# First K and V on GpSimd's queue, ahead of the zero fills, and one late fill moved off SyncE's queue

## The chip, the cores and the metric

The kernel runs on one core of a Trainium2 chip. The metric is the device time of one execution in microseconds, the median of several. Executions of one kernel on one chip lie within about 0.4% of each other. All data movement of the core goes through 16 DMA engines. Three instruction streams start transfers on them: SyncE (queue q1 in the profile), GpSimd (q0, which the profile calls software_dynamic) and ScalarE (q10, little used here).

## The reference, cut

One decode step of a pre-norm transformer layer, forward and backward. Attention sees the last 4096 of 32768 cached positions, 8 K/V heads of 256:

```
k = k_cache[:, :, Sk - W:, :]; v = v_cache[:, :, Sk - W:, :]     # W = 4096, Sk = 32768
p = softmax(q @ k.T / 16);  h = x + (p @ v) @ wo
h2 = h + ((ln(h) @ w_gate) * (ln(h) @ w_up)) @ w_down
out = h2, and the gradients of x, k_cache, v_cache, wq, wo, w_gate, w_up, w_down
```

The gradients of the caches have the full shape (1, 8, 32768, 256) in bf16, and seven eighths of each are zeros. Writing 235 MB of zeros is most of this kernel's work.

## The kernel before

Zeros are written from one area of SBUF, `zeros` (128 x 8192 bf16, 16 KB a partition). Its second half is lent to a weight block for a while. The parts that matter, with cuts marked:

```python
    nc.vector.memset(ar(0, ZW // 2), 0.0)               # ZW = 8192; LD = nc.sync, ZQ = nc.gpsimd
    nc.gpsimd.memset(ar(ZW // 2, ZW // 2), 0.0)
    LD.dma_start(out=wqA, in_=wq_A)                     # query weights, 3.1 MB and 0.5 MB
    LD.dma_start(out=wqB, in_=wq_B)
    LD.dma_start(out=x_bf[:], in_=...)
    # ...
    late_jobs = [(out_2, G - 1, 5, 7, 2 * ZW), (out_3, G - 1, 0, 6, 2 * ZW), (out_3, G - 1, 6, 7, ZW)]
    # fills: 2 MB pieces, 7 to a (gradient, head); for head 7 only 5 pieces of out_2
    send_fills(0, HALF0)                 # 42 pieces in 6 DMAs of 14 MB, packets of 16 KB
    send_fills(HALF0, HALF1, True)       # 15 pieces from the first half of the source, packets of 8 KB
    # ...
    load_kv(K_off[0], A_k_cache, 0)      # on SyncE, 2.1 MB
    LD.dma_start(out=dh2_bc[:], in_=grad_out...)
    load_kv(V_off[0], A_v_cache, 0)
    # ... attention, then the gated block in three weight blocks:
    for n in range(len(BLOCKS)):
        # ... products of block n; block 1's gate and up weights lie in the second half of the zero source
        if n + 2 < len(BLOCKS):
            load_block(n + 2)
        if n == 1:
            nc.vector.memset(ar(ZW // 2, ZW // 2), 0.0)      # give the half back
            send_fills(HALF1, len(fills) - 1)                # the other 16 KB fills, on GpSimd
    # ... backward of attention; then the last fill in four odd DMAs, then on SyncE:
    for o, g, n0, n1, f in late_jobs:
        # ... zero fills behind the last outputs
```

Of the kernel before, what the change touches and what calls it, by code (L numbers as in the profile page):

```python
# [16 lines left out]
G = 8  # L17
Dh = 256
W = 4096
T = 32  # L20
# [3 lines left out]
Sk = 32768  # L24
EPS = 1e-5
SCALE = 1.0 / 16.0
ZW = 8192
HALF0, HALF1 = 42, 57
GROUP = 7
NZ = (Sk - W) * Dh // (128 * ZW)  # L30
KB = 512
# [3 lines left out]
def kernel(  # L35
        ctx, tc, A_x, A_k_cache, A_v_cache, A_wq, A_wo, B_x, B_w_gate, B_w_up, B_w_down, grad_out,
           out_0, out_1, out_2, out_3, out_4, out_5, out_6, out_7, out_8):
    nc = tc.nc
    LD = nc.sync
    ZQ = nc.gpsimd  # L40
# [10 lines left out]
    MB = UB + 48 * KB  # L51
# [3 lines left out]
    def ar(off, n):  # L55
        return arena[:, off:off + n]

    def kv_at(off):
        return ar(off, T * Dh).rearrange("p (t d) -> p t d", d=Dh)

    zeros = ar(0, ZW)
    A_off = [VB, VB + 32 * KB, UB + 32 * KB, UB, UB + 16 * KB, VB + 16 * KB]
    V_off = [A_off[i] for i in (0, 1, 2, 3, 4, 5, 0, 1)]
    K_off = [RB, RB + 32 * KB, MB + 16 * KB, RB, RB + 32 * KB, A_off[1], RB, RB + 32 * KB]
# [28 lines left out]
    dg_bc = ar(A_off[5], 2 * F).rearrange("p (i f) -> p i f", i=2)  # L93
    diag2 = ar(A_off[5] + 2 * F, F)

    nc.vector.memset(ar(0, ZW // 2), 0.0)
    nc.gpsimd.memset(ar(ZW // 2, ZW // 2), 0.0)
    x_bf = const.tile([1, D], bf16)
    dh2_bc = const.tile([128, D], bf16)
    wq_A = A_wq[0:384, :].rearrange("(c p) j -> p c j", c=3)  # L100
# [17 lines left out]
        reg = o[0, g, 0:Sk - W, :].rearrange("s d -> (s d)")[n0 * 128 * ZW:n1 * 128 * ZW]  # L118
        return reg.rearrange("(n p f) -> n p f", p=128, f=f)

    late_jobs = [(out_2, G - 1, 5, 7, 2 * ZW), (out_3, G - 1, 0, 6, 2 * ZW), (out_3, G - 1, 6, 7, ZW)]
    fills = []
    for g in range(G):
        for o in (out_2, out_3):
            if g == G - 1 and o is out_3:
                continue
            fills += [(o, g, i) for i in range(5 if g == G - 1 else NZ)]

    def send_fills(n0, n1, halves=False):
        while n0 < n1:  # L130
# [72 lines left out]
        nc.vector.scalar_tensor_tensor(out=r[:], in0=t[:], scalar=rstd, in1=plus, op0=ALU.mult, op1=ALU.add)  # L203
        return r

    def load_kv(off, cache, g):
        LD.dma_start(out=kv_at(off), in_=cache[0, g, Sk - W:, :].rearrange("(p t) d -> p t d", t=T))

    load_kv(K_off[0], A_k_cache, 0)
    LD.dma_start(out=dh2_bc[:], in_=grad_out.rearrange("a b d -> (a b) d").to_broadcast([128, D]))  # L210
    load_kv(V_off[0], A_v_cache, 0)
    load_kv(K_off[1], A_k_cache, 1)
    load_kv(V_off[1], A_v_cache, 1)

    dup = small.tile([1, 128], bf16, tag="dup", bufs=1)
    nc.vector.tensor_copy(out=dup[:].rearrange("o (m w) -> o m w", w=2), in_=x_bf[:, 384:D].unsqueeze(2).to_broadcast([1, 64, 2]))
# [18 lines left out]
                                 start=False, stop=(h == 1 and k == 2))  # L235
    qT_bf = const.tile([128, 32], bf16)
    nc.vector.tensor_copy(out=qT_bf[:], in_=qT_ps[:])
    load_kv(K_off[2], A_k_cache, 2)
    load_kv(V_off[2], A_v_cache, 2)

    pT_all = const.tile([128, G, T, 2], bf16)
    oT_f = const.tile([128, 2, H], f32)
# [30 lines left out]
    with tc.tile_pool(name="ps_m", bufs=1, space=bass.MemoryType.PSUM) as ps_m, \  # L273
# [43 lines left out]
        def moments(g, p_f):  # L317
            K_sb, V_sb = kv_at(K_off[g]), kv_at(V_off[g])
            M_ps = ps_m.tile([128, 2, 2 * Dh], f32, tag="M")
            for c in range(8):  # L320
                pK = pK_slot[c % 2]
                nc.vector.tensor_tensor(out=pK, in0=K_sb[:, 4 * c:4 * c + 4, :].unsqueeze(2).to_broadcast([128, 4, 2, Dh]),  # L322
                                        in1=p_f[:, c::8, :].unsqueeze(3).to_broadcast([128, 4, 2, Dh]), op=ALU.mult)
                for i in range(4):
                    t = 4 * c + i
                    for vh in range(2):
                        nc.tensor.matmul(M_ps[:, vh, :], lhsT=V_sb[:, t, vh * 128:(vh + 1) * 128], rhs=pK[:, i, :, :].rearrange("p h d -> p (h d)"),  # L327
                                         start=(t == 0), stop=(t == T - 1))
            for t in range(T):
                nc.tensor.matmul(ok_ps[:].rearrange("p k d -> p (k d)"), lhsT=ppad[g % 2][:, 8 * (t % 4) + t // 4, :], rhs=both(g, t),  # L330
                                 start=(g == 0 and t == 0), stop=(g == G - 1 and t == T - 1))
            for vh in range(2):
                nc.scalar.copy(out=M_sb[g][:, vh].rearrange("p h d -> p (h d)"), in_=M_ps[:, vh, :])  # L333

        def load_wo(n):
            LD.dma_start(out=wo_sb[:, 16 * n:16 * n + 16, :], in_=A_wo.rearrange("(p j) n -> p j n", j=32)[:, 16 * n:16 * n + 16, :])
# [4 lines left out]
        for g in range(G):  # L341
            p_f = p_next
            if g + 1 < G:
                p_next = scores(g + 1)
            moments(g, p_f)
            for kind, n in after.get(g, []):
                if kind == "K":
                    load_kv(K_off[n], A_k_cache, n)
                else:
                    load_kv(V_off[n], A_v_cache, n)  # L350
            if g == G - 2:
                load_wo(0)
        nc.vector.tensor_copy(out=ok_rows, in_=ok_ps[:])
# [151 lines left out]
    with tc.tile_pool(name="work2", bufs=2) as work2, tc.tile_pool(name="lnw", bufs=1) as lnw, \  # L505
# [10 lines left out]
                                     start=False, stop=(kh == 1))  # L516
            nc.scalar.activation(out=dq_bc[:, g * 512:(g + 1) * 512], in_=dqb_ps[:, 0, :], func=ACT.Copy, scale=SCALE)  # L517
        for g in range(2):
            load_kv(MB + 16 * KB * g, A_v_cache, g)

        HJ = H * Dh // 2
        dn1 = lnw.tile([128, 5], f32)
# [92 lines left out]
        for it, g in enumerate(order):  # L615
# [30 lines left out]
            for l in range(8):  # L646
                for qp in range(2):
# [5 lines left out]
                    t = 4 * l + 2 * qp  # L653
# [14 lines left out]
        o, g, i = fills[-1]  # L668
        flat = zero_rows(o, g, i, i + 1, ZW)[0].rearrange("p f -> (p f)")
        base = 0  # L670
        for p0, k, m, w in ((0, 5, 2, 288), (20, 3, 8, ZW), (64, 8, 9, ZW - 40), (0, 4, 8, ZW)):
            n = k * m * w
            ZQ.dma_start(out=flat[base:base + n].rearrange("(k m f) -> k m f", k=k, m=m),
                         in_=zeros[p0:p0 + 4 * k - 3:4, 0:w].unsqueeze(1).to_broadcast([k, m, w]))
# [35 lines left out]
```

## Time and profile before

| | kernel before |
|---|---|
| time, median | 793.49 us (793.19 to 794.0, 4 runs) |
| profiled execution | span 791.1 us |
| bytes moved | 334.75 MB: q0 216.01, q1 116.68 |
| rate in the long middle (60 to 300 us) | 430 GB/s |

The quantity used is **lost time**: a moment t, less the bytes moved until then divided by 430 GB/s. It is worked out from the packet records of the trace. A flat stretch of it is a stretch in which the DMA engines are full. As the rate hardly rises above 430 GB/s anywhere, a step is time that isn't made up later. The profile's lines are shown in the prediction below.

### The profile page before, as it was taken

To read this page: it belongs to the slowest core of one execution; us is meant where nothing else is said; L and a number is where in the kernel's file an instruction comes from. 1 tells how busy PE (TensorE), PEld (TensorE's weight loads), DVE (VectorE), ACT (ScalarE), POOL (GpSimd) and SP (SyncE) were. 2 spreads that over 40 slices of the span, in tenths; PEclk is the share of its full clock that TensorE was granted. 3 is DMA by queue.
4 is the path that set the end of the run, shared out by engine and by line. 5 is a ranking of instruction groups with operands and counts; after the bars stand their busy time and mean duration, and the time that the engine had idled before them with its cause. 6 is when DMAs were issued, how large, how long until landed. Compare 5 with 4: busy or idle time off the path is not lost.

```text
span 791.1 us, 7239 instructions
## 1 busy us (share of the span) xinstructions
PE 475.9 (60%) x2926; PEld 220.8 (28%) x2926; DVE 410.6 (52%) x621; ACT 196.1 (25%) x309; POOL 29.8 (4%) x41
## 2 busy tenths in 40 slices
PE   0359998999999999453226848583551535363100
PEld 0224333344343433142114714231210211131000
DVE  2105764847658476052884288486680583555300
ACT  0043123141241301000101207372331344134300
POOL 6000000000000000110300000000000000001000
PEclk9987999999999999655556959886556556556555
DMA  9999999999999999999999999999999999999998
GB/s 345 429 432 430 429 430 431 432 431 432 428 427 430 427 427 426 418 420 422 433 431 425 425 425 432 427 429 430 427 426 429 428 427 429 423 428 407 413 439 350
DMA packets 28759, 334.75 MB, mean 423 GB/s; under 512 B 1966, under 2 KB 5046, under 8 KB 6966
## 3 DMA queue, kind: packets, MB, share of 16 engines
q0 software_dynamic: 15904, 216.01, 64.2%
q1 hardware_dynamic: 11382, 116.68, 35.1%
q10 hardware_dynamic: 1440, 1.61, 0.6%
q8 instruction: 23, 0.38, 0.2%
q14 instruction: 10, 0.08, 0.0%
HBM read 53.69 MB, written 280.59 MB: 423 GB/s over the span
## 4 chain that ended last, share of the span: by engine, by line
another core or an unknown queue 40%; DMA 25%; DVE 14%; PE 10%; issue 2%; POOL 2%; ACT 1%; DVEq 0%; ACTq 0%; SPq 0%; POOLq 0%
DMA out_dram<-arena 25%; DVE arena L469 2%; PE rows_ps L266 2%; DVE arena L658 2%; DVE arena L554 2%; PE dqb_ps L512 2%; DVE arena L659 2%; PE d_ps L651 2%; PE tr_ps L263 1%; DVE arena L524 1%; DVE arena L438 1%; POOL out_dram L138 1%; PE dqb_ps L515 1%; DVE arena L623 1%
## 5 line engine op out<-in xcount | busy, mean ns | idle before, releaser
L322 DVE TENSOR_TENSOR arena<-arena,p_f 128x2048 bf16<-128x2048 bf16 x64 | 145.4, 2287 | 64.3 <-PE M_ps L327 64.2
L327 PE MATMUL M_ps<-arena 128*128 128x512 bf16 x512 | 129.3, 381 | 0.2 <-ACT arena L333 0.2
L651 PE MATMUL d_ps<-arena 32*128 32x512 bf16 x256 | 45.4, 521 | 100.6 <-DVE arena L659 85.7
L263 PE MATMUL tr_ps<-ident_bf,arena 128*128 128x128 bf16 x1024 | 92.2, 241 | 20.2 <-DMA arena<-in_A_k_cache_dram 12.7
L266 PE MATMUL rows_ps<-arena,vpad 128*16 128x512 bf16 x256 | 89.5, 445 | 21.4 <-DVE arena L623 15.9
L263 PEld LDWEIGHTS <-arena 128*128 128x128 bf16 x1024 | 68.3, 107 | 74.2 <-issue 60.3
L280 ACT COPY arena<-tr_ps 128x1024 bf16<-128x1024 bf16 x64 | 61.8, 1015 | 70.5 <-PE tr_ps L263 70.5
L330 PE MATMUL ok_ps<-arena 128*16 128x512 bf16 x256 | 64.0, 381 | 0.9 <-DVE arena L307 0.9
L655 ACT CAST arena<-d_ps 128x512 bf16<-128x512 f32 x64 | 37.7, 589 | 106.1 <-PE d_ps L651 106.1
L327 PEld LDWEIGHTS <-arena 128*128 128x128 bf16 x512 | 43.3, 99 | 59.2 <-issue 23.4
L621 ACT COPY arena<-tr_ps 128x1024 bf16<-128x1024 bf16 x32 | 32.5, 1016 | 109.9 <-PE tr_ps L263 35.8
L658 DVE CAST arena<-d_ps 128x512 bf16<-128x512 f32 x64 | 43.9, 686 | 18.2 <-PE d_ps L651 17.7
L659 DVE CAST arena<-d_ps 128x512 bf16<-128x512 f32 x64 | 43.6, 681 | 15.5 <-DMA out_dram<-arena 15.5
L651 PEld LDWEIGHTS <-arena 32*128 32x128 bf16 x256 | 10.7, 96 | 126.0 <-issue 81.9
L656 ACT CAST arena<-d_ps 128x512 bf16<-128x512 f32 x64 | 38.1, 595 | 16.8 <-DMA out_dram<-arena 16.8
L266 PEld LDWEIGHTS <-vpad 128*16 128x16 bf16 x256 | 18.7, 91 | 58.4 <-issue 50.6
L330 PEld LDWEIGHTS <-arena 128*16 128x16 bf16 x256 | 19.1, 89 | 41.6 <-issue 20.5
L549 DVE TENSOR_SCALAR arena<-arena,xT 128x1792 bf16<-128x1792 bf16 (+1 forms) x9 | 7.7, 881 | 37.1 <-DMA out_dram<-arena 37.1
L295 ACT ACTIVATE e_f<-cols_ps,nbias 128x32 f32<-128x32 f32 x16 | 4.5, 286 | 86.9 <-DVE nbias L291 86.9
L524 DVE CUSTOM_DVE_ANT_0 arena<-arena 128x4096 bf16<-128x4096 bf16 x3 | 13.1, 4421 | 23.7 <-ACT arena L517 23.7
L268 DVE COPY arena<-rows_ps 16x512 f32<-16x512 f32 x16 | 10.8, 676 | 27.7 <-PE rows_ps L266 27.7
L623 DVE COPY arena<-tr_ps 128x1024 bf16<-128x1024 bf16 x32 | 21.8, 683 | 3.0 <-PE tr_ps L263 2.5
(198 smaller groups left out, 382.2 us busy)
## 6 DMA issues: line engine op xcount, KB each, us to landing
out_dram<-arena POOLq DMA_DIRECT2D x11, 14336.0 KB, 196.1
out_dram<-arena SPq DMA_DIRECT2D x18, 2048.0 KB, 25.6
out_dram<-arena POOLq DMA_DIRECT2D x15, 2048.0 KB, 54.2
arena<-in_A_v_cache_dram SPq DMA_DIRECT2D x10, 2048.0 KB, 52.8
arena<-in_A_k_cache_dram SPq DMA_DIRECT2D x8, 2048.0 KB, 31.3
out_dram<-arena SPq DMA_DIRECT2D x4, 4096.0 KB, 26.1
out_dram<-arena POOLq DMA_DIRECT2D x1, 12288.0 KB, 43.0
out_dram<-arena POOLq DMA_DIRECT2D x1, 8192.0 KB, 337.3
```

Source lines behind the costliest of these rows:

```text
L263: nc.tensor.transpose(tr_ps[:, dh, i, :], X_sb[:, 4 * q + i, dh * 128:(dh + 1) * 128], ident_bf[:])
L266: nc.tensor.matmul(rows_ps[:], lhsT=pad[:, dh, 16 * q:16 * q + 16], rhs=XT[:, dh].rearrange("p t k -> p (t k)"), start=(q == 0 and dh == 0 ...
L280: sT_ps = dots(kv_at(K_off[g]), KT_slot, vpad[g % 2], rows1, ps_c, "cols", lambda q, XT, ps: nc.scalar.copy(out=XT, in_=ps))
L322: nc.vector.tensor_tensor(out=pK, in0=K_sb[:, 4 * c:4 * c + 4, :].unsqueeze(2).to_broadcast([128, 4, 2, Dh]), in1=p_f[:, c::8, :].unsqueez ...
L327: nc.tensor.matmul(M_ps[:, vh, :], lhsT=V_sb[:, t, vh * 128:(vh + 1) * 128], rhs=pK[:, i, :, :].rearrange("p h d -> p (h d)"), start=(t == ...
L330: nc.tensor.matmul(ok_ps[:].rearrange("p k d -> p (k d)"), lhsT=ppad[g % 2][:, 8 * (t % 4) + t // 4, :], rhs=both(g, t), start=(g == 0 and ...
L621: nc.scalar.copy(out=XT, in_=ps)
L651: nc.tensor.matmul(d_ps[:, qi].rearrange("p w d -> p (w d)"), lhsT=rTm[32 * q:32 * (q + 1), l, :], rhs=R_sb[32 * q:32 * (q + 1), :], start ...
L655: nc.scalar.copy(out=stV[:, t:t + 2, :], in_=d_ps[:, :, 0, :])
L656: nc.scalar.copy(out=stK[:, t:t + 2, :], in_=d_ps[:, :, 1, :])
L658: nc.vector.tensor_copy(out=stV[:, t:t + 2, :], in_=d_ps[:, :, 0, :])
L659: nc.vector.tensor_copy(out=stK[:, t:t + 2, :], in_=d_ps[:, :, 1, :])
```

## The change

The intent is to let K and V of head 0 arrive earlier by a queue that is otherwise waiting, and to keep GpSimd's queue running longer while the last outputs are computed. For that, one zero fill of 4 MB (pieces 5 and 6 of `out_2`, head 7; "the late fill" from here on) goes from SyncE's tail to GpSimd. The core of the diff (the other calls of `load_kv` only get the engine as an argument):

```diff
-    nc.vector.memset(ar(0, ZW // 2), 0.0)
-    nc.gpsimd.memset(ar(ZW // 2, ZW // 2), 0.0)
+    load_kv(ZQ, K_off[0], A_k_cache, 0)
+    load_kv(ZQ, V_off[0], A_v_cache, 0)
+    nc.vector.memset(zeros, 0.0)
...
-    late_jobs = [(out_2, G - 1, 5, 7, 2 * ZW), (out_3, G - 1, 0, 6, 2 * ZW), (out_3, G - 1, 6, 7, ZW)]
+    late_jobs = [(out_3, G - 1, 0, 6, 2 * ZW), (out_3, G - 1, 6, 7, ZW)]
...
-            fills += [(o, g, i) for i in range(5 if g == G - 1 else NZ)]
+            fills += [(o, g, i) for i in range(NZ)]
...
-    load_kv(K_off[0], A_k_cache, 0)
     LD.dma_start(out=dh2_bc[:], in_=grad_out...)
-    load_kv(V_off[0], A_v_cache, 0)
```

More of the change, by code (lines that the diff above doesn't have):

```diff
@@ L94, with load_kv @@
     diag2 = ar(A_off[5] + 2 * F, F)
-    nc.vector.memset(ar(0, ZW // 2), 0.0)
-    nc.gpsimd.memset(ar(ZW // 2, ZW // 2), 0.0)
+    def load_kv(eng, off, cache, g):
+        eng.dma_start(out=kv_at(off), in_=cache[0, g, Sk - W:, :].rearrange("(p t) d -> p t d", t=T))
+    load_kv(ZQ, K_off[0], A_k_cache, 0)
+    load_kv(ZQ, V_off[0], A_v_cache, 0)
+    nc.vector.memset(zeros, 0.0)
     x_bf = const.tile([1, D], bf16)
@@ L204, in layernorm_bwd @@
         return r
-    def load_kv(off, cache, g):
-        LD.dma_start(out=kv_at(off), in_=cache[0, g, Sk - W:, :].rearrange("(p t) d -> p t d", t=T))
-    load_kv(K_off[0], A_k_cache, 0)
     LD.dma_start(out=dh2_bc[:], in_=grad_out.rearrange("a b d -> (a b) d").to_broadcast([128, D]))
-    load_kv(V_off[0], A_v_cache, 0)
-    load_kv(K_off[1], A_k_cache, 1)
-    load_kv(V_off[1], A_v_cache, 1)
+    load_kv(LD, K_off[1], A_k_cache, 1)
+    load_kv(LD, V_off[1], A_v_cache, 1)
     dup = small.tile([1, 128], bf16, tag="dup", bufs=1)
@@ L237 @@
     nc.vector.tensor_copy(out=qT_bf[:], in_=qT_ps[:])
-    load_kv(K_off[2], A_k_cache, 2)
-    load_kv(V_off[2], A_v_cache, 2)
+    load_kv(LD, K_off[2], A_k_cache, 2)
+    load_kv(LD, V_off[2], A_v_cache, 2)
     pT_all = const.tile([128, G, T, 2], bf16)
@@ L347 @@
                 if kind == "K":
-                    load_kv(K_off[n], A_k_cache, n)
+                    load_kv(LD, K_off[n], A_k_cache, n)
                 else:
-                    load_kv(V_off[n], A_v_cache, n)
+                    load_kv(LD, V_off[n], A_v_cache, n)
             if g == G - 2:
@@ L518 @@
         for g in range(2):
-            load_kv(MB + 16 * KB * g, A_v_cache, g)
+            load_kv(LD, MB + 16 * KB * g, A_v_cache, g)
         HJ = H * Dh // 2
```

## The prediction

> **What bounds the kernel now.** I read the slices of the page first, then the queues, then the engines in stretches, and only then single instructions. The page says that the 16 DMA engines are busy in all 40 slices, and how many bytes they move:
>
> ```profile
> DMA  9999999999999999999999999999999999999998
> GB/s 345 429 432 430 429 430 431 432 431 432 428 427 430 427 427 426 418 420 422 433 431 425 425 425 432 427 429 430 427 426 429 428 427 429 423 428 407 413 439 350
> DMA packets 28759, 334.75 MB, mean 423 GB/s; under 512 B 1966, under 2 KB 5046, under 8 KB 6966
> ...
> q0 software_dynamic: 15904, 216.01, 64.2%
> q1 hardware_dynamic: 11382, 116.68, 35.1%
> ```
>
> The reader is to see 334.75 MB at about 430 GB/s, which is 778 us of pure moving, in a span of 791. So the kernel is bound by the sum of its bytes, and a change can only win or lose **time in which the DMA engines are not full**. Of the two queues, q0 is GpSimd's (zero fills, 216 MB) and q1 is SyncE's. The table by stretches says where the 12.6 us beyond 778 lie:
>
> ```profile
> 0.00:10.00 10.00, 0.37 (x1) 0.09 (x1) 4.55 (x18) 1.28 (x1) 9.41 (x14) 1.00 0.84 283
> 10.00:60.00 50.00, 18.72 (x224) 12.24 (x225) 4.60 (x21) 10.41 (x15) 2.64 (x4) 0.94 1.00 426
> 60.00:300.00 240.00, 235.00 (x1322) 95.64 (x1319) 153.16 (x139) 65.51 (x98) 3.41 (x5) 0.98 1.01 430
> 300.00:375.00 75.00, 41.33 (x248) 21.15 (x247) 26.68 (x60) 5.45 (x12) 5.46 (x8) 0.66 1.02 421
> ...
> 740.00:745.00 5.00, 0.76 (x8) 0.11 (x4) 2.58 (x4) 2.15 (x4) 0.00 (x0) 0.50 0.84 353
> 745.00:785.00 40.00, 0.00 (x0) 0.00 (x0) 0.00 (x0) 0.00 (x0) 0.00 (x0) 0.50 1.01 432
> 785.00:791.00 6.00, 0.00 (x0) 0.00 (x0) 0.00 (x0) 0.00 (x0) 0.00 (x0) 0.50 0.46 194
> ```
>
> The last two columns are DMA share and GB/s. At the start 283 against 430 for 10 us is 3.4 us lost; at 740 to 745, 0.9 us; at the end 3.3 us, the last transfers and their landing. TensorE is full from 60 to 300 (235 of 240 us), but no DMA waits for it there: zero fills take whatever rate the loads leave.
>
> One stage is fragile. The second half of the zero source is lent to a weight block, so GpSimd sends fills from the first half only (15 fills of 2 MB in 8 KB packets) until VectorE has zeroed the second half again. The timelines of TensorE, VectorE and GpSimd there:
>
> ```profile
> 372.34 0.74 PE L420 MATMUL gu_ps<-X_b,arena 64*128 64x1 bf16 x8 [1.67 <-DMA arena<-in_B_w_gate_dram]
> 381.23 1.76 DVE L443 MEMSET arena<- 128x2048 uint32 x1 [0.41 <-DVE hh_f L424]
> 383.29 5.71 POOL L142 DMA_DIRECT2D out_dram<-arena  x6 [30.72 <-DVE arena L443]
> ```
>
> Weights land at 372, the memset ends at 383.0, the next fills are issued at 383.3. The packet records show their first 16 KB packet at 389.7, while most engines finish their last 8 KB packet between 389.5 and 391.5. From 375 to 400 q1 carries nothing. So the new fills come with about one microsecond to spare: the same release some microseconds later leaves the DMA engines empty.
>
> **What the Trainium skill says.** "DMA: Bandwidth & Descriptors", section "Specifications", gives 435 GB/s as the ceiling of the fabric and about 358 GB/s as an HBM limit. The trace agrees with the first (430 held for hundreds of microseconds) and contradicts the second. The same page, "Issuing engines are not separate DMA queues": transfers started by scalar, sync or gpsimd run on the same 16 engines and interleave. The trace agrees (the shares of q0 and q1 add up to 99.3% of 16 engines), so moving a transfer to another queue buys no bandwidth. The same page, "Queues, rings and completion order": each engine takes turns between queues packet by packet. The trace agrees: between 16 and 20 us, q0 with 16 KB packets moves 328 GB/s beside q1 with mostly 4 KB packets at 108. Hence **small packets get a small share**. "Specifications" also gives about 1 us to the first byte of a GpSimd DMA; here it was 5.7 us (issued at 5.13, first q0 packet at 10.82), and 5.2 us at 715.
>
> **The change part by part.**
>
> (1) K and V of head 0 (2.1 MB each) leave q1 and go first into q0. They are issued at about 0.75 us, so with 5.5 us of latency they move from 6.3 us on. The bytes are the same. q1 alone already reached 430 GB/s from 4 to 7 us, so the only start time to be won is the dip from 7.5 to 12 us, where the rate fell to 246 to 311 GB/s: 0.6 MB, 1.4 us. If that dip comes from GpSimd's writing the fills' descriptors (5 to 12 us), it stays. I take **-0.7 us**.
>
> (2) The zero source is now cleared by VectorE alone: twice the 1.76 us memset, 3.5 us, ending near 4.8 instead of GpSimd's 4.25. Fills wait behind K and V anyway: 0.
>
> (3) The compute chain. Weights wq now share with 16 KB packets from 6.3 us, at one third of the rate (estimate 142 GB/s), so x and grad_out, queued behind them, come at about 25 (now 21) and 32 us (now 37.9, as K no longer stands ahead). In the built program TensorE now transposes K before this and waits for grad_out before the query product, so the first scores end near 47 (now 51). Then it gains more: now TensorE idles 5 us for the second K until 58.5, which will land near 42. The first weighted product of VectorE starts at 61.5 now, about 51 then: a **lead of 10 us**. By itself worth nothing, as the DMA is the bound.
>
> (4) The order of loads in the weight stage. The instruction order of the built program shows that the gate and up weights of block 1 (the ones in the borrowed half) now stand behind those of block 2 on SyncE's and ScalarE's queues. Block 2's wait for VectorE to be done with block 0 (issued at 355.4 now). So block 1's loads no longer run while block 0 is computed. With the lead of 10 us, shrunk to 8.5 by 16 KB fills that last until about 309, block 2's loads go out near 347, land after the 15 to 17 us they take now, near 364, and block 1's need another estimate of 11.6 us: 28 packets per engine in turn with an 8 KB fill packet, 0.415 us a turn. They land at 375. Then come the products of block 1 (2.7), broadcast and copies (5.2 in block 0 now), the four products of 1.23 (4.9) and the memset (1.8): **end at 389.5 instead of 383.0**.
>
> (5) What that costs. By bytes the 8 KB fills end at the same moment as now, 389.5 to 391.5, less the 0.7. New fills would flow from 389.5 + 5.5 = 395. The DMA engines stand idle for about **+5 us**, and nothing makes that up.
>
> (6) The late 4 MB fill leaves SyncE's tail (18.9 MB of q1 lie behind the last outputs, now from 743) and lengthens q0, which now ends at 730. That keeps DMA engines full while the last outputs are computed, so the dip at 740 to 745 should go: **-0.9 us**. The end itself stays.
>
> Sum: -0.7 + 5 - 0.9 = +3.4, so about 797.
>
> **The rivals.** *The intent works*: the weights land in time, there is no gap, and only -0.7 to -2.3 is left: 791 to 793. For it: the lead may be larger than 10 us, and 5 us more would close the gap; (4) is a sum of nine terms. Against it: the slack now is only about 1 us. *The gap is larger*: a lead of 5 us, or small packets that starve beside 16 KB fills, puts the memset at 395 and the gap at 10 us, 802; beyond 15 us would need the lead to vanish. *Compute becomes the bound at the end*: the chain leaves the weight stage some 6 us later than now, and q0 keeps half the rate until nearly 740, so the last outputs may come after q0 has run dry: +3 to +6 on top. Against: q0's extra 4.2 MB covers 10 us. *All hidden*: the start is shared differently and nothing else moves: 793.
>
> **Range and chances.** Everything here is a few microseconds out of 793; 2% is 15.9. The intent alone gives 791, the gap with a late tail about 803. I take 797 with 790 to 804. Faster by 2% needs 16 us of empty DMA time, and there are only 12.6 in all: 1%. Slower by 2% needs a gap of 17 us or more: 4%. Within 2%: 95%.
>
> **What would show it.** Right: the first q0 packets near 6 us, x later than 21 us, the first weighted product near 51, TensorE's waits for K shorter; in the weight stage a wait for the block 1 gate or up weights at about 375, the memset ending near 389, and a slice near 390 with a DMA share clearly under 9 and GB/s well under 420; no dip at 740. Wrong: the memset ending by 383 with full slices (the intent), or full slices near 390 and a hole near 740 (the tail). The prediction fails most likely at the lead of (3), or at how block 1's loads queue in (4).

## The result, and the profile after

The kernel after took **794.15 us** (median of 4, 793.5 to 794.7) against 793.49. The ratio is 1.0007 with a 95% interval of 0.999 to 1.0025. A ratio here is the mean time of one kernel's fast runs over that of the other's of the same rounds, so it is not quite the ratio of the medians. So the two kernels are the same within what can be measured. The page of the kernel after, its slices and its queues:

```profile
DMA  9999999999999999999999999999999999999997
GB/s 361 412 428 430 430 433 428 430 432 428 431 429 426 433 420 416 428 422 421 430 432 419 427 426 429 430 427 433 423 426 429 426 427 431 423 427 418 419 437 324
DMA packets 28871, 334.75 MB, mean 422 GB/s; under 512 B 1950, under 2 KB 5030, under 8 KB 6950
...
q0 software_dynamic: 16448, 224.40, 66.8%
q1 hardware_dynamic: 10950, 108.29, 32.4%
```

The same bytes, 8.4 MB of them on the other queue, and still full slices. The first slice is higher than before (361 against 345), the second lower (412 against 429): something was won and given back at once. The table by stretches:

```profile
0.00:10.00 10.00, 0.00 (x0) 0.00 (x0) 4.71 (x11) 1.28 (x1) 6.93 (x15) 1.00 0.83 319
10.00:60.00 50.00, 26.06 (x290) 16.00 (x292) 10.94 (x34) 16.80 (x21) 2.62 (x4) 1.00 1.01 417
...
740.00:745.00 5.00, 1.63 (x12) 0.22 (x8) 3.15 (x5) 2.68 (x6) 0.00 (x0) 0.50 1.05 423
745.00:785.00 40.00, 0.61 (x4) 0.11 (x4) 2.01 (x4) 1.62 (x4) 0.00 (x0) 0.50 1.01 429
785.00:792.00 7.00, 0.00 (x0) 0.00 (x0) 0.00 (x0) 0.00 (x0) 0.00 (x0) 0.50 0.40 171
```

In such a table the columns are the stretch, its length, the busy time of PE, PEld, DVE, ACT and POOL, the granted clock, the DMA share and GB/s. The start gained (319 against 283) and 10 to 60 us lost (417 against 426). The dip at 740 to 745 us is gone (423 against 353), but the end is thinner (171 GB/s over 7 us). The predicted gap would lie near 390 us. The timelines of TensorE, VectorE and GpSimd there:

```profile
371.10 2.38 PE L419 MATMUL gu_ps<-X_b,arena 64*128 64x1 bf16 x29 [1.47 <-DMA arena<-in_B_w_gate_dram]
382.76 1.76 DVE L442 MEMSET arena<- 128x2048 uint32 x1 [0.41 <-DVE gu_f L420]
384.82 5.65 POOL L146 DMA_DIRECT2D out_dram<-arena  x6 [31.26 <-DVE arena L442]
```

The weights land at 371.1, the memset ends at 384.5 and the next fills are issued at 384.8. That is 1.5 us later than before, not 6.5. The slices, of the kernel before and then of the kernel after, show no gap:

```profile
385.00:390.00 5.00, 3.03 (x20) 2.06 (x19) 3.40 (x10) 1.50 (x3) 3.99 (x5) 0.50 1.03 434
390.00:395.00 5.00, 0.69 (x2) 0.11 (x1) 3.64 (x6) 1.02 (x3) 0.78 (x1) 0.50 1.02 436
```

```profile
385.00:390.00 5.00, 3.23 (x14) 1.45 (x15) 4.90 (x18) 1.73 (x3) 5.00 (x6) 0.50 1.03 434
390.00:395.00 5.00, 1.75 (x14) 1.16 (x11) 3.23 (x4) 0.79 (x3) 1.32 (x2) 0.50 1.01 433
```

The packet records add a telling detail. The first 16 KB packet of these fills starts at 389.7 us in both kernels, although in the kernel after it was issued 1.5 us later. So that moment is not a latency counted from the issue. The new fills stand in the same queue behind the 8 KB fills and start when their turn comes.

Lost time at marks of the profiled executions (us; the two parts of the change alone are the first two experiments):

| at | 10 | 16 | 24 | 200 | 410 | 700 | 785 | last packet | lost after 785 |
|---|---|---|---|---|---|---|---|---|---|
| before | 3.6 | 4.2 | 4.2 | 4.2 | 6.1 | 8.0 | 9.7 | 11.2 | 1.5 |
| after | 2.8 | 2.8 | 4.2 | 4.4 | 6.4 | 8.6 | 9.8 | 12.4 | 2.6 |
| kv_only | 2.9 | 2.9 | 4.3 | 4.4 | 6.4 | 8.7 | 10.3 | 11.6 | 1.3 |
| late_only | 3.7 | 4.3 | 4.3 | 4.5 | 6.5 | 8.2 | 9.3 | 11.4 | 2.1 |

Four statements can be read off. By 16 us the kernel after is 1.4 us ahead; by 24 us it has lost all of that. Spread thinly from 24 to 700 us it loses 0.7 us more than before. From 700 to 785 us it loses 0.6 us less (1.1 against 1.7), most of it where the dip at 740 us went. After 785 us it loses 1.1 us more, because the 16 engines end unevenly: in the kernel before 16 packets are in flight until 787.6 us, in the kernel after 14 at 786 and 11 at 787.5. (The packet records name no engine, so which of them end late can't be read.) The sum, +1.2 us, is the difference of these two executions (794.31 against 793.07); the medians differ by 0.7. The loss between 24 and 700 us stands in kv_only too and hardly in late_only. But in the records of fill_late and warm_late (below), whose K and V stay on SyncE's queue, about 1.1 us more is lost in that stretch than in the kernel before, so the queue of K and V isn't its only cause.

### The profile page after: what moved, and what is told of

Same layout as the page of the kernel before. It is cut to its first block, busy times and chain, and to the rows that moved or that the text cites. A ratio compares the mean times of both kernels' runs of the same rounds, so it can differ in the third digit from the quotient of the medians.

```text
span 792.4 us, 7212 instructions
## 1 busy us (share of the span) xinstructions
PE 464.1 (59%) x2903; PEld 217.6 (27%) x2926; DVE 411.8 (52%) x621; ACT 196.0 (25%) x309; POOL 27.1 (3%) x42
## 4 chain that ended last, share of the span: by engine, by line
another core or an unknown queue 40%; DMA 27%; DVE 14%; PE 9%; issue 2%; ACT 1%; POOL 1%; DVEq 0%; ACTq 0%; SPq 0%; POOLq 0%
DMA out_dram<-arena 25%; DMA arena<-in_A_v_cache_dram 3%; DVE arena L468 2%; DVE arena L657 2%; PE dqb_ps L511 2%; DVE arena L553 2%; PE rows_ps L265 2%; DVE arena L658 2%; PE d_ps L650 2%; PE tr_ps L262 1%; DVE arena L523 1%; PE dqb_ps L514 1%; DVE arena L437 1%; DVE arena L622 1%
## 5 line engine op out<-in xcount | busy, mean ns | idle before, releaser
L326 PE MATMUL M_ps<-arena 128*128 128x512 bf16 x489 | 125.7, 380 | 1.9 <-issue 0.8
L262 PE MATMUL tr_ps<-ident_bf,arena 128*128 128x128 bf16 x1024 | 88.3, 233 | 20.1 <-DMA arena<-in_A_k_cache_dram 14.0
L265 PE MATMUL rows_ps<-arena,vpad 128*16 128x512 bf16 x256 | 85.6, 430 | 21.8 <-DVE arena L622 16.1
L262 PEld LDWEIGHTS <-arena 128*128 128x128 bf16 x1024 | 65.1, 104 | 70.3 <-issue 55.1
L326 PEld LDWEIGHTS <-arena 128*128 128x128 bf16 x512 | 43.3, 99 | 59.6 <-issue 23.6
L650 PEld LDWEIGHTS <-arena 32*128 32x128 bf16 x256 | 10.8, 95 | 133.5 <-issue 82.4
L419 PE MATMUL gu_ps<-X_b,arena 128*128 128x1 bf16 x112 | 9.7, 186 | 33.2 <-DMA arena<-in_B_w_gate_dram 32.2
L267 DVE COPY arena<-rows_ps 16x512 f32<-16x512 f32 x16 | 10.8, 676 | 29.0 <-PE rows_ps L265 29.0
```

The lines of the kernel that those rows point to most:

```text
L262: nc.tensor.transpose(tr_ps[:, dh, i, :], X_sb[:, 4 * q + i, dh * 128:(dh + 1) * 128], ident_bf[:])
L265: nc.tensor.matmul(rows_ps[:], lhsT=pad[:, dh, 16 * q:16 * q + 16], rhs=XT[:, dh].rearrange("p t k -> p (t k)"), start=(q == 0 and dh == 0 ...
L326: nc.tensor.matmul(M_ps[:, vh, :], lhsT=V_sb[:, t, vh * 128:(vh + 1) * 128], rhs=pK[:, i, :, :].rearrange("p h d -> p (h d)"), start=(t == ...
L650: nc.tensor.matmul(d_ps[:, qi].rearrange("p w d -> p (w d)"), lhsT=rTm[32 * q:32 * (q + 1), l, :], rhs=R_sb[32 * q:32 * (q + 1), :], start ...
```

## The experiments

All runs gave a correct result. The three groups ran on three chips (kv_only to mem9; fill_first to x_first; the last three), so each run is compared with the kernel before on its own chip, and across chips only within the scatter.

**kv_only: the first part of the change alone.** The kernel after, with the two lines of the late fill as before.

```diff
-    late_jobs = [(out_3, G - 1, 0, 6, 2 * ZW), (out_3, G - 1, 6, 7, ZW)]
+    late_jobs = [(out_2, G - 1, 5, 7, 2 * ZW), (out_3, G - 1, 0, 6, 2 * ZW), (out_3, G - 1, 6, 7, ZW)]
-            fills += [(o, g, i) for i in range(NZ)]
+            fills += [(o, g, i) for i in range(5 if g == G - 1 else NZ)]
```

> Only K and V of head 0 move to GpSimd's queue; the late 4 MB fill stays on SyncE's. Theory (ends of the span): the start is won and lost again within the first 30 us, so the time stays within 0.5 us of the kernel before (793.5), with a rate near 319 GB/s in the first 10 us, a dip to about 365 GB/s between 18 and 24 us, and q0 done near 730 to 735 as before. Rival (the start is a gain of 0.8 us, the tail takes it back): 792.7, faster than the whole change by 1.5 us. Rival of the prediction (a gap in the weight stage): the release of the 16 KB fills comes at about 384.8 here too; a gap would show as a slice near 390 below 400 GB/s.

Measured: 794.19 us against 793.22, ratio 1.0015 (1.0001 to 1.0028). The part alone brings nothing; if anything it costs a microsecond.

**late_only: the second part alone.** The kernel before, with the same two lines as in the kernel after (the diff above, reversed).

> Only the late 4 MB fill moves; K and V of head 0 stay with SyncE. The order of the weight loads is that of the kernel before. Theory (ends of the span): the dip at 740 to 745 (353 GB/s before) goes, a gain of 0.8 us, but the last transfers of the 16 engines end less evenly, a loss of about 0.9 us: time within 0.5 us of before. Rival (the tail dip is a pure gain): 792.6. Rival (the tail costs more than it brings): 794.5, and then this part alone makes the 0.7 us by which the whole change is slower.

Measured: 793.34 us, ratio 1.0001 (0.9988 to 1.0013). The dip at 740 us goes here too, and the end is less even (2.1 us lost after 785 us against 1.5).

**mem3 and mem9: is there a cliff near 390 us, and where?** The kernel after, with the memset that frees the borrowed half done three or nine times, which delays GpSimd's next fills by a known amount.

```diff
-                nc.vector.memset(ar(ZW // 2, ZW // 2), 0.0)
+                for _ in range(3):        # 9 in mem9
+                    nc.vector.memset(ar(ZW // 2, ZW // 2), 0.0)
```

> The changed kernel with the zeroing memset of the weight stage done three times instead of once (same result), so that the fills from the whole source are released some 4 to 5 us later. Theory (the release stood at the edge, with 0 to 2 us of slack): the DMA engines run dry after the 8 KB fills, q0 moves nothing for 2 to 5 us near 391 to 394, and the time grows by 2 to 5 us to 796 to 799. Rival (fills are elastic and the stage has room): no gap, time as the changed kernel, 794.2.

> As the run with three memsets, with nine: the release comes some 17 to 20 us later. Theory (edge, then one for one): a gap of 15 to 20 us, and the time grows by the same, to 809 to 814, unless compute's lag is partly absorbed. Rival (room of 10 us or more in this stage): less than half of that, under 803. Third (all is elastic): 794.2.

mem3 took 794.24 us (ratio 1.0011), the same as the kernel after, so its expected 796 to 799 was wrong and its rival right. GpSimd's timeline and the slice at 390 us:

```profile
390.71 6.48 POOL L146 DMA_DIRECT2D out_dram<-arena  x7 [37.04 <-DVE arena L443]
```

```profile
390.00:395.00 5.00, 2.84 (x8) 0.66 (x9) 4.16 (x14) 1.16 (x3) 4.29 (x5) 0.50 0.92 369
```

Here the memset ended at 390.4 us, 0.9 us after the moment that the prediction gave for the kernel after (389.5), and the loss is not 5 us. Lost time rises by 1.0 us from 390 to 410 us, and it is too small to see in the time.

mem9 took 811.26 us (ratio 1.0225):

```profile
407.22 6.48 POOL L146 DMA_DIRECT2D out_dram<-arena  x7 [53.80 <-DVE arena L443]
```

```profile
390.00:395.00 5.00, 0.00 (x0) 0.00 (x0) 4.25 (x7) 0.00 (x0) 0.00 (x0) 0.50 0.41 174
395.00:400.00 5.00, 0.00 (x0) 0.00 (x0) 4.22 (x7) 0.00 (x0) 0.00 (x0) 0.50 0.01 5
400.00:410.00 10.00, 4.48 (x17) 1.51 (x18) 9.25 (x12) 2.52 (x5) 2.78 (x4) 0.50 0.18 74
```

The engines run dry, and 16.5 us of lost time between 390 and 410 us in the records are 17.1 us in the time, over the kernel after: one for one. The mechanism of the prediction is real. From this run comes the size of the reserve. The first packet of the delayed fills starts at 408.6 us, **1.4 us** after the issue (in mem3 also 1.4, 392.2 after 390.7). So the 8 KB fills were used up at 408.6 - 16.5 = 392.1 us. This is a mean over the engines: most end by 393, a last one only at 395.9. In the kernel after, packets could have come from an estimated 384.8 + 1.4 = 386.2 us on. By this the reserve was 5.9 us there and 7.4 us in the kernel before, not one.

**fill_first and fill_late: what is the dip that moved?** In the kernel before the rate dips at 7.5 to 12 us, in the kernel after at 18 to 21 us. One run puts one 2 MB fill between K and V, the other lets the fills wait for the query weights.

```diff
# fill_first, on the kernel after
-    load_kv(ZQ, K_off[0], A_k_cache, 0)
-    load_kv(ZQ, V_off[0], A_v_cache, 0)
...
-    send_fills(0, HALF0)
+    send_fills(0, 1)
+    load_kv(ZQ, K_off[0], A_k_cache, 0)
+    load_kv(ZQ, V_off[0], A_v_cache, 0)
+    send_fills(1, HALF0)
# fill_late, on the kernel before, in place of the two memsets of the zero source
+    nc.vector.tensor_scalar(out=zeros, in0=ar(MB, ZW), scalar1=0.0, scalar2=None, op0=ALU.mult)
```

In the source the first fill stands ahead of K. In the trace GpSimd issues K at 1.68 us, the fill at 5.45 and V at 6.00, which is the order that was wanted.

> The kernel after, with one zero fill of 2 MB moved ahead of V's load on GpSimd's queue (order K, one fill, V, the other fills). It asks what the dip of some 1.4 us of lost traffic is that lies at 8 to 11.5 us in the kernel before and at 18 to 21 us in the kernel after. T1, the dip belongs to the first zero fill, the first write to DRAM: it moves to about 10 to 14 us, where K ends and the first fill begins, and 18 to 21 us are near 430 GB/s. T2, it belongs to what SyncE's queue does (the end of the first weight load and the start of the next): it stays at 17 to 21 us, and 10 to 14 us are near 430 GB/s. In both the time is that of the kernel after within 0.3% (about 794.2 us): the same bytes through the same 16 engines.

> The kernel before, with the zeros made by VectorE from the first weight load (times 0), so that the fills can only start when that load has landed; K and V of the first head on SyncE's queue as before. T1 (the dip belongs to the first zero fill): none at 8 to 11.5 us, where one queue of loads alone should keep near what it had, and a dip of about 1.4 us within 3 us of the first fill's packets. T2 (it belongs to SyncE's loads): it stays near 8 to 11.5 us although no fill runs. If SyncE's queue alone keeps the 16 engines full, the time is that of the kernel before plus 0 to 1 us (793.5 to 794.5); if it does not, the loss in those first us comes on top, one for one.

Measured: fill_first 795.48 us (ratio 1.0015, 0.9996 to 1.0034), fill_late 794.37 (1.0002, 0.9985 to 1.0019), against 793.75 for the kernel before. The stretches of the kernel before, of the kernel after, of fill_first and of fill_late:

```profile
5.00:10.00 5.00, 0.37 (x1) 0.09 (x1) 1.55 (x7) 0.00 (x0) 4.98 (x6) 1.00 1.03 359
10.00:16.00 6.00, 0.00 (x0) 0.00 (x0) 0.00 (x0) 0.00 (x0) 2.64 (x4) 1.00 0.96 391
16.00:24.00 8.00, 1.00 (x6) 0.85 (x7) 1.86 (x9) 0.29 (x1) 0.00 (x0) 1.00 1.02 435
```

```profile
5.00:10.00 5.00, 0.00 (x0) 0.00 (x0) 1.38 (x11) 0.00 (x0) 4.56 (x5) 1.00 1.02 428
10.00:16.00 6.00, 0.82 (x6) 0.55 (x6) 0.00 (x0) 0.00 (x0) 1.95 (x3) 1.00 1.00 426
16.00:24.00 8.00, 0.00 (x0) 0.00 (x0) 0.00 (x0) 0.00 (x0) 0.67 (x1) 1.00 1.02 367
```

```profile
10.00:16.00 6.00, 0.00 (x0) 0.00 (x0) 0.00 (x0) 0.00 (x0) 1.22 (x2) 1.00 1.00 351
16.00:24.00 8.00, 0.00 (x0) 0.00 (x0) 0.00 (x0) 0.00 (x0) 1.66 (x2) 1.00 1.01 428
```

```profile
10.00:16.00 6.00, 1.01 (x7) 0.87 (x8) 4.06 (x10) 0.29 (x1) 2.63 (x3) 1.00 1.04 438
16.00:24.00 8.00, 8.00 (x143) 5.52 (x142) 0.78 (x6) 2.02 (x2) 4.86 (x6) 1.00 0.93 340
```

The low stretch goes where the first zero fill goes: 5 to 16 us, 16 to 24, 10 to 16, 16 to 24. In each trace it begins two to three microseconds ahead of the first fill's packets (10.8, 19.8, 14.0 and 19.3 us), ends at the latest two microseconds after them, and costs 1.1 to 1.7 us in these four. fill_late alone would prove little, since 114 of the gradient row's 128 packets of 896 bytes run at 16 to 18 us, and little else does. The cleanest case is sp_late, described next. SyncE's first packet comes at 16.6 us there, the first fill's at 13.2, and the low stretch lies between:

```profile
12.00:14.00 2.00, 1.56 (x19) 1.38 (x18) 2.00 (x18) 1.80 (x3) 0.00 (x0) 1.00 0.98 287
```

The DMA share stays near 1 there: the engines count as busy, but single packets take longer (for 16 KB at 18 to 21 us of the kernel after a median of 1039 ns and up to 1439, against 611). The theory that it belongs to SyncE's weight loads falls. So does the thought of the prediction that it comes with GpSimd's writing of the descriptors. The first six fills are issued at 5.4 to 11.3 us in the kernel after, where the rate is 426 to 428. fill_first is 1.3 us slower than the kernel after, on another chip, which is inside the 0.3% that was expected and not clear of the scatter. In its profiled execution it loses 0.8 us more after 785 us and 1.2 us more spread between 60 and 700 us, and neither is explained.

**sp_late: when is GpSimd's queue slow to start?** The kernel after, with all first loads of SyncE held back by memsets of their targets.

```diff
     nc.vector.memset(zeros, 0.0)
+    nc.vector.memset(ar(MB, 28 * KB), 0.0)       # targets of wqA and wqB
...
+    nc.vector.memset(x_bf[:], 0.0)
+    nc.vector.memset(dh2_bc[:], 0.0)
+    for off in [K_off[1]] + V_off[1:6]:
+        nc.vector.memset(kv_at(off)[:, 0, 0:2], 0.0)
```

> The kernel after, with every first load of SyncE's queue held back to about 10 to 12 us by memsets of its targets on VectorE, so that GpSimd's K and V go out into an otherwise idle DMA system at the same 1.3 us. L1 (GpSimd's queue is slow to its first packet only where SyncE's packets already fill the engines, 4.2 to 5.7 us against the 1.3 us that the releases at 391 and 407 us showed): K's first packet starts at 2.4 to 3.2 us. L2 (the first use of that queue in a program is slow by itself): it starts at 5.0 to 6.0 us as in the kernel after. Time: 0 to 5 us over the kernel after by how much of the first 12 us one queue leaves unused; under L1 the first 16 us lose about 2 to 3 us in all, so 793 to 795.

Measured: 794.58 us (ratio 1.0004, 0.9988 to 1.0021). SyncE's first packet came at 16.6 us, later than the 10 to 12 that were meant. K is issued at the same moment as in the kernel after, beside an empty SyncE queue:

```profile
1.31 0.70 POOL L97 DMA_DIRECT2D arena<-in_A_k_cache_dram  x1 [0.86 <-POOLq L698]
```

Its first packet starts at 2.7 us, **1.4 us** after the issue. In the kernel after it took 4.4 us (issued at 1.30, first packet at 5.65), beside SyncE loads that grew to 426 GB/s. In x_first, where SyncE moved less than 200 GB/s until then, it took 2.6 (1.31, 3.92). For the first fill it was 5.9 us in fill_late (13.37, 19.25) and 5.7 in the kernel before, beside a SyncE queue at over 400 GB/s in the first half of that time, with the dip in the second. So the wait for the first packet belongs to the company, and not to the first use of the queue. How SyncE's packets bring it about isn't shown.

**x_first: does the lead of compute count?** The kernel after, with the input row and the gradient row ahead of the query weights on SyncE's queue.

```diff
+    LD.dma_start(out=x_bf[:], in_=A_x...)
+    LD.dma_start(out=dh2_bc[:], in_=grad_out...to_broadcast([128, D]))
     LD.dma_start(out=wqA, in_=wq_A)
```

(The two later loads of the same rows are taken out.)

> The kernel after, with the input row and the gradient row loaded ahead of the query weights on SyncE's queue. It makes their landing and perhaps the compute lead earlier, not the bytes fewer. The theory that the 16 DMA engines bound the kernel from end to end expects the same time as the kernel after within 0.2% (794.2 us, 793.4 to 795.0), whatever the lead of compute; a theory in which the early compute chain still counts expects 1 us or more less.

Measured: 794.14 us (ratio 1.0001, 0.9987 to 1.0014), the time of the kernel after. The last weighted product of the attention ends at 307.1 us in the kernel before, 292.7 in the kernel after, 292.5 in x_first, 311.9 in sp_late and 287.1 in fill_late. x_first itself moved that end by only 0.2 us and so tests little; fill_late and sp_late are the test. Compute that runs 20 us ahead of the kernel before or 5 us behind it leaves the time within 793.5 to 794.6 us.

**warm_after, warm_late and late_only_b: can the dip be sent where it costs nothing?** If the dip belonged to the program's first write to DRAM, a tiny write at 1 us would draw it into the first 5 us, where the engines are not full anyway. On the kernel after, and on late_only, the fastest of the changed kernels so far (its expectation below calls it the fastest of all, but the kernel before took 793.22 us beside it), which was run again beside it unchanged (late_only_b):

```diff
+    nc.vector.memset(ar(0, 256), 0.0)
+    nc.scalar.dma_start(out=out_2[0, 0, 0:32, :], in_=ar(0, 256)[0:32])
-    nc.vector.memset(zeros, 0.0)
+    nc.vector.memset(ar(256, ZW - 256), 0.0)     # warm_late: ar(256, ZW // 2 - 256) in VectorE's memset
```

> The kernel after, with one 16 KB write of zeros to the output (32 rows of 512 bytes) sent by ScalarE's queue at about 1 us, long before GpSimd's first zero fill, which still waits behind K and V. fill_first, fill_late, sp_late and x_first showed a dip of 0.7 to 1.7 us of lost traffic in the two to three us ahead of the first zero fill, wherever that stands. W1, the dip belongs to the first write of the program to DRAM: it moves into the first 5 us, where the engines are not full anyway, and 16 to 24 us go from 367 GB/s to above 420; the lost time at 24 us falls from 4.04 to about 2.7 to 3.2, and the time by 0.8 to 1.4 us to about 793.0. W2, it belongs to the first big fill of GpSimd's queue and not to a write as such: it stays at 18 to 21 us and the time stays at 794.2.

> The kernel before with only the late fill moved (the fastest of the kernels so far at 793.34), with the same early 16 KB write. W1: the dip at 8 to 11.5 us goes, and the time falls by 0.8 to 1.4 us to about 792.2, which would beat both kernels by a little. W2: dip and time stay, 793.3.

> The kernel before with only the late fill moved, once more, as the neighbour of the run above on the same chip. Expected: 793.3 within 0.4 us, ratio to before 0.9995 to 1.0005; its tail (lost time after 785 us) shows whether the uneven end of the 16 engines, 2.1 us in its first profile against 1.5 before, is the same in another execution or differs from run to run.

Measured: warm_after 793.84 us (ratio 1.0007, 0.9994 to 1.0021), warm_late 793.08 (0.9998, 0.9985 to 1.001), late_only_b 793.35 (1.0004, 0.9991 to 1.0017), all against 793.47. The early write ran at 4 to 5.5 us (512-byte packets on ScalarE's queue), and the dip stayed ahead of the first fill. The stretches of warm_after and of warm_late:

```profile
16.00:24.00 8.00, 0.00 (x0) 0.00 (x0) 0.00 (x0) 0.00 (x0) 0.67 (x1) 1.00 0.98 352
```

```profile
10.00:16.00 6.00, 0.14 (x3) 0.15 (x3) 0.17 (x2) 0.00 (x0) 4.13 (x5) 1.00 1.01 362
```

So the dip is not tied to the first write. It comes with the first big fill of GpSimd's queue, and why is open. None of the versions beats the kernel before by more than the scatter.

The uneven end was the same in both executions of late_only (2.1 us lost after 785 us in each). But over all kernels with the late fill moved it goes from 1.2 (mem3) over 1.5 (sp_late) to 3.5 us (fill_first), and in fill_late, where the late fill was not moved, it is 3.1. The move alone does not set it. What does is open.

## Why the prediction was wrong

The class, the range and the bound were right, but the time was not. The prediction forecast +3.4 us, and +0.7 was measured, which is within the scatter. By its own steps:

1. *Start, -0.7.* The dip was to be won, at a guess by half. In fact K and V filled it: 1.4 us by 16 us. The first q0 packet came at 5.65 us, near the predicted 6.3, but by luck: it was issued 0.55 us later and waited 1.1 us less than assumed. Then the dip came back at the first fill, so the net is 0. The reservation that the loss might stay was right, and its reason (descriptor writing) was not.
2. *Zero source, 0.* Right.
3. *Lead of compute, 10 us at the first product.* It was 5.9 there (55.6 against 61.5) and grew to 14.4 us by the last weighted product (292.7 against 307.1). The input row landed at 27.6 us (25 predicted) and the gradient row at 33.7 (32 predicted). The estimate of 142 GB/s for SyncE beside 16 KB packets held: 131 to 163 from 6 to 12 us.
4. *Load order of the weight blocks.* Its length was right: block 2's loads were issued at 343.4 us and block 1's gate weights landed at 371.1, 27.7 us later (28 predicted). Its start was not, because the lead there was 12.0 us and not 8.5. With 1.1 us less for the work of block 1, the memset ended at 384.5 us instead of 389.5: **5.0 us**.
5. *The gap, +5.* **This is the step that failed**: "New fills would flow from 389.5 + 5.5 = 395. The DMA engines stand idle for about +5 us". The 5.5 us was read as a fixed latency of GpSimd's queue from places where it is something else: at the start a wait beside a full SyncE queue, and before 390 us the turn behind older fills in the same queue. Its figure of 5.2 us at 715 was taken beside a SyncE queue at 350 to 436 GB/s too. At 390 us SyncE carries almost nothing, and there the runs measured 1.4 us. Counted from the issue 0.3 us after the memset, that is **3.8 us** less. Together the new fills could flow 8.8 us earlier than predicted (386.2 against 395.0), ahead of the 392.1 us at which the old ones run out. The reserve of "about one microsecond", read off at the same place, was 7.4 us by mem9. Step 4's error alone would have been enough to close the gap (384.8 + 5.5 = 390.3). Step 5's alone nearly so: mem3 put the memset 0.9 us past the predicted moment, and lost 1.0 us in place of 5.
6. *Tail, -0.9.* The dip at 740 us went as predicted. From 700 to 785 us that was worth 0.6 us, and "the end itself stays" was wrong: the engines ended unevenly and lost 1.1 us more than before.

So the rival that came nearest is "all hidden" (793), by its number; that "nothing else moves" was not so. The range held because it also covered the case without a gap. The intent was met at the start and at 740 us, and both gains were returned a few microseconds later. The 0.7 us that the kernel after loses more between 24 and 700 us are not explained.

## What to carry to other kernels

In a kernel bound by its bytes, only time in which the engines are not full can be won, so follow lost time along the span, and look for each gain again a few microseconds later. Before a delay between issue and first packet is used as a latency, ask what stood ahead in the same queue and what filled the engines from the other: here the same queue needed 1.4 us or 5.9. And size a reserve by delaying its release on purpose by two amounts. Two such runs gave it to within a microsecond, where reading one trace gave one microsecond instead of six to seven.

## What the Trainium skill lacked or had wrong

- "DMA: Bandwidth & Descriptors", section "Specifications": about 1 us to the first byte on GpSimd's path. Beside an empty SyncE queue it was 1.4 us in mem3, mem9 and sp_late, which is near. Beside SyncE loads it was 2.6 to 5.9 us, which that section does not say.
- The same page and section: about 358 GB/s as the HBM limit of a core. The kernel held 430 GB/s for hundreds of microseconds. The page's section "Measured (HBM→SBUF, 128 partitions, SWDGE, issued from GpSimd)" says that its figures are of a single core with its neighbour idle (425 GB/s at 16 MB), and the prediction, which called this a contradiction, should have read that. The table derives the limit as half of a stack's 716 GB/s, and does not say that one core alone can go above it.
- The same page, section "Two DMAs through the same engine are not ordered": within one queue of one engine, descriptors start in order. The trace agrees (first 16 KB packet at 389.7 us whether issued at 383.3 or 384.8). What it lacks is the warning that this turn in the queue looks like latency in a trace.
- No page that was read has the dip of 0.7 to 1.7 us at the first large fill of GpSimd's queue, in which 16 KB packets take up to 1439 ns in place of 611.
